# Linear attention and two feed-forward layers: decay products by two long scans per tile, the state kept scaled

## The chip, the cores and the metric

The kernel runs on one core of a Trainium2 chip. TensorE (PE, its weight loads PEld), VectorE (DVE), ScalarE (ACT) and GpSimd (POOL) each work through their own queue in order; SyncE (SP) issues DMAs. The metric is device time in microseconds (us), and a profiled execution gives the trace.

## The reference

A linear attention with a decay per channel runs over 768 steps of 4 sequences and 8 heads of width 48. Its output, 3072 rows of 384, passes two feed-forward layers (FFN).

```python
for t in range(S):                                   # S = 768, D = 48
    cur = einsum('bhd,bhe->bhde', u * k[t], v[t])
    y[t] = einsum('bhd,bhde->bhe', r[t], state + cur)
    state = w[t][..., None] * state + einsum('bhd,bhe->bhde', k[t], v[t])
x = y as rows                                        # 3072 x 384
h = x @ w_in;  x = (h * clip(h + 3, 0, 6) / 6) @ w_out          # d_ff 2048
h = x @ w_in2; s = h * softmax(h); x = layernorm(s) * g_ln @ w_out2   # d_ff 1024
```

The decays w of the inputs lie between 0.8 and 0.95. The weights come as 64-bit floats and are decoded on the chip.

## The kernel before

**Tiles.** The sequence is cut into chunks of 128 steps. A tile is one chunk of one sequence: 6 chunks by 4 sequences make 24 tiles, numbered chunk first, so that tiles 0 to 3 are the first chunk of the four sequences and tile i+4 follows tile i in time. Four tiles of one chunk make a group, and a group feeds 16 FFN slots of 512 columns; slot n multiplies with block m = n mod 16 of the first FFN's weights.

**Stages of a tile.** `stw` clamps the decays to 0.75 to 1.25 (tile wc; on VectorE for tiles 0 to 3, on GpSimd after) and lets ScalarE add up how far any decay lies outside (tile junk), which in the end picks a fallback. `st0` turns w and r (tiles wt, rt in PSUM, by TensorE for tiles 0 to 9, by a VectorE transpose, `flip`, for tiles 10 to 23) and makes the decay products: q by four backward scans of 128 (one for each pair of heads), its reciprocal at the chunk's start, e by four forward scans of 127, and then e times rt. `st1` multiplies q with the turned keys (kt) and makes z = r k u on GpSimd (tile r), whose sum d is taken on VectorE. `keys_in` turns q k back (ktp, ktok), `scores` makes the score products (pa) and the masked scores: GpSimd writes the diagonal (am), VectorE copies pa over it (L630). `state_add` makes the new state, `out_x` the tile's output yt and its high and low parts xh and xl.

**State.** `state_in` makes, on GpSimd, sp = state times the chunk's whole decay (the first column of q) and sr, the columns 32 to 48 of the same. `out_x` multiplies e with sp and sr, and `state_add` adds the keys' product to sp (L649).

**FFN and decode.** `ffn_in` makes h (L720), t and gh (L724 to L726), `ffn_low` gl (on GpSimd in slots 0 to 15, on VectorE after); `ffn_out` follows two slots later (L745), and after a group's last slot ScalarE writes ye (L751) and issues its three stores (L752). Block m of the weights is loaded by `w1_load` (three buffers, raw), decoded on ScalarE (L63) and VectorE (L66, L50, L53), and split (ScalarE L71, VectorE L72). From slot 0 on, one block is decoded in each slot until all 16 are done.

**Order.** SP's queue is in the order of the code, as is GpSimd's until the first FFN slot; the other engines' instructions, and GpSimd's from then on, are put in order by the scheduler that builds the kernel. Every engine then keeps its order, so that an instruction that waits holds all behind it.

After 96 slots the second FFN (L950, L964, L977) goes over the 24 tiles with rows that `load_y` reads back.

Of the kernel before, what the change touches and what calls it, by code (L numbers as in the profile page):

```python
# [278 lines left out]
def fast_path(  # L279
# [107 lines left out]
    at = {}  # L387
    x_t = {}
# [102 lines left out]
    def stw(i):  # L491
        a = at[i]
        if i >= LATE:
            x = late["w"][:, :, 0:4 * D - 16]
            junk = atp.tile([P, HP, 4 * D - 16], mybir.dt.uint8, tag="junk", name="junk", bufs=1)
            nc.scalar.activation(
                out=junk, in_=x, func=ACTF.Relu, scale=-1.0, bias=b_lo, accum_out=chk[:, 3 * i:3 * i + 1]
            )
            nc.scalar.activation(
                out=junk, in_=x, func=ACTF.Relu, bias=b_hi, accum_out=chk[:, 3 * i + 1:3 * i + 2]  # L500
            )
            nc.gpsimd.tensor_scalar(out=x, in0=x, scalar1=W_HI, scalar2=W_LO, op0=ALU.min, op1=ALU.max)
# [8 lines left out]
        a["wc"] = wc  # L511
        junk = atp.tile([P, H, D], BF16, tag="junk", name="junk", bufs=1)
# [7 lines left out]
    def st0(i):  # L520
        a = at[i]
        g = i // B
        if i < LATE:
            wt = ps_in(i, "wt", "y0")
            trans(wt, a["wc"])
            rt = ps_in(i, "rt", "y1")
            trans(rt, a["r"])
        else:
            wt, rt = flip("w"), flip("r")
        q = atp.tile([P, HP, C + 1], F32, tag="q", name="q")  # L530
        e = atp.tile([P, HP, C], F32, tag="e", name="e")
        nc.gpsimd.memset(q[0:DP, :, C:C + 1], 1.0)
# [12 lines left out]
        a.update(q=q, e=e)  # L545

    def st1(i):
# [6 lines left out]
        else:  # L554
            kt = flip("k")
# [8 lines left out]
    def state_in(i):  # L564
        a = at[i]
        b = i % B
        q = a["q"]
        sp = atp.tile([P, HP, 2 * D], F32, tag="sp", name="sp", bufs=1)
# [3 lines left out]
        sr = atp.tile([P, HP, 32], F32, tag="sr", name="sr", bufs=1)  # L572
        nc.gpsimd.tensor_tensor(
            out=sr[0:DP].rearrange("p h (j d) -> p h j d", j=2),
            in0=s_st[b][0:DP].rearrange("p h (j d) -> p h j d", j=2)[:, :, :, 32:D],
            in1=q[0:DP, :, 0:1].unsqueeze(3).to_broadcast([DP, HP, 2, D - 32]), op=ALU.mult,
        )
        a["sp"], a["sr"] = sp, sr
# [53 lines left out]
    def state_add(i):  # L632
# [5 lines left out]
        for h in range(H):  # L638
# [97 lines left out]
    def ffn_out(n):  # L736
# [118 lines left out]
    for tick in range(starts[-1] + NS):  # L855
# [8 lines left out]
        for m in decodes.get(tick, []):  # L864
# [17 lines left out]
    for n in range(NSLOT + LAG):  # L882
# [45 lines left out]
    load_y(0)  # L928
    load_y(1)
# [113 lines left out]
```

## Time and profile before

| what | value |
|---|---|
| median of 3 runs | 775.6 us (774.93 to 776.07) |
| the profiled execution | 774.71 us, span 772.6 us |
| PE busy | 733.3 us (95%) |
| DVE busy | 535.1 us (69%) |
| ACT busy | 333.1 us (43%) |
| POOL busy | 266.3 us (34%) |
| granted TensorE clock, mean | 0.971 of full speed |

The span runs from the first instruction to the last; 2.1 us of the profiled time lie around it. Busy times overlap. A slice of the page is a fortieth of the span, 19.3 us: TensorE is at 5 to 8 tenths in the first seven slices, and at 9 or more in nearly all the others.

### The profile page before, as it was taken

To read this page: it belongs to the slowest core of one execution; us is meant where nothing else is said; L and a number is where in the kernel's file an instruction comes from. 1 tells how busy PE (TensorE), PEld (TensorE's weight loads), DVE (VectorE), ACT (ScalarE), POOL (GpSimd) and SP (SyncE) were. 2 spreads that over 40 slices of the span, in tenths; PEclk is the share of its full clock that TensorE was granted. 3 is DMA by queue.
4 is the path that set the end of the run, shared out by engine and by line. 5 is a ranking of instruction groups with operands and counts; after the bars stand their busy time and mean duration, and the time that the engine had idled before them with its cause. 6 is when DMAs were issued, how large, how long until landed. Compare 5 with 4: busy or idle time off the path is not lost. (4 is left out here: it accounts for less than half of the span.)

```text
span 772.6 us, 14109 instructions
## 1 busy us (share of the span) xinstructions
PE 733.3 (95%) x5308; PEld 620.9 (80%) x5308; DVE 535.1 (69%) x1012; ACT 333.1 (43%) x647; POOL 266.3 (34%) x397
## 2 busy tenths in 40 slices
PE   5778797999999999999999999999999999999996
PEld 4556685888887888878888888888899999999995
DVE  6979889658777777777787865787555555555552
ACT  3455456334434333433334334654444444444442
POOL 5556547742332333333333311224322222222200
PEclk9669998999999999999999999999999999999998
DMA  9794754534344344443335203422111111111001
GB/s 168 172 172 124 178 133 101 108 86 97 86 95 121 86 104 87 93 117 82 91 74 130 63 1 103 144 94 70 65 48 44 41 42 48 45 42 42 31 22 36
DMA packets 151405, 67.31 MB, mean 87 GB/s; under 512 B 101792, under 2 KB 145952, under 8 KB 151328
## 3 DMA queue, kind: packets, MB, share of 16 engines
q1 hardware_dynamic: 148736, 61.60, 33.6%
q10 hardware_dynamic: 2592, 4.72, 1.6%
q8 instruction: 44, 0.72, 0.4%
q14 instruction: 33, 0.27, 0.1%
HBM read 56.33 MB, written 9.44 MB: 85 GB/s over the span
## 5 line engine op out<-in xcount | busy, mean ns | idle before, releaser
L745 PE MATMUL y<-gh,w_h 128*128 128x512 f32 x288 | 115.8, 402 | 0.0
L720 PE MATMUL h<-xh,w_h 128*128 128x512 f32 x288 | 113.4, 394 | 0.0
L720 PE MATMUL h<-xl,w_h 128*128 128x512 f32 x288 | 113.1, 393 | 0.0
L745 PE MATMUL y<-gl,w_h 128*128 128x512 f32 x288 | 113.1, 393 | 0.0
L745 PE MATMUL y<-gh,w_l 128*128 128x512 f32 x288 | 113.0, 392 | 0.0
L720 PE MATMUL h<-xh,w_l 128*128 128x512 f32 x288 | 112.7, 391 | 0.0
L726 ACT ACTIVATE gh<-t 128x512 fp32r<-128x512 f32 x96 | 60.4, 629 | 116.4 <-DVE t L725 116.4
L724 ACT ACTIVATE t<-h,cols 128x512 f32<-128x512 f32 x96 | 65.2, 680 | 93.2 <-PE h L720 91.2
L725 DVE SCALAR_TENSOR_TENSOR t<-t,h 128x512 f32<-128x512 f32 x96 | 65.1, 678 | 34.6 <-ACT t L724 34.3
L734 DVE TENSOR_TENSOR gl<-t,gh 128x512 fp32r<-128x512 f32 x80 | 66.7, 834 | 24.1 <-ACT gh L726 19.1
L78 DVE TENSOR_REDUCE nm<-h 128x1 f32<-128x1024 f32 x24 | 29.4, 1225 | 61.5 <-PE h L950 61.4
L977 PE MATMUL po<-w_oh,qh 128*128 128x384 f32 x192 | 67.2, 350 | 0.3 <-ACT qh L966 0.3
L745 PEld LDWEIGHTS y<-gh,w_h 128*128 128x128 f32 x288 | 54.3, 189 | 13.9 <-issue 3.2
L977 PE MATMUL po<-w_oh,ql 128*128 128x384 f32 x192 | 64.8, 337 | 0.1
L977 PE MATMUL po<-w_ol,qh 128*128 128x384 f32 x192 | 64.8, 338 | 0.0
L745 PEld LDWEIGHTS y<-gh,w_l 128*128 128x128 f32 x288 | 54.5, 189 | 11.8
L720 PEld LDWEIGHTS h<-xh,w_h 128*128 128x128 f32 x288 | 54.6, 190 | 11.5
L720 PEld LDWEIGHTS h<-xh,w_l 128*128 128x128 f32 x288 | 54.6, 190 | 11.4
L720 PEld LDWEIGHTS h<-xl,w_h 128*128 128x128 f32 x288 | 54.6, 190 | 11.3
L745 PEld LDWEIGHTS y<-gl,w_h 128*128 128x128 f32 x288 | 54.6, 190 | 10.4
L966 ACT ACTIVATE qh<-pt 128x512 fp32r<-128x512 f32 x48 | 26.1, 595 | 78.4 <-PE pt L964 78.4
L950 PE MATMUL h<-w_ih,yl 128*128 128x512 f32 x144 | 56.4, 392 | 0.0
(132 smaller groups left out, 1482.6 us busy)
## 6 DMA issues: line engine op xcount, KB each, us to landing
raw<-in_moe_w_out_dram SPq DMA_DIRECT2D x24, 384.0 KB, 6.2
raw<-in_moe_w_in_dram SPq DMA_DIRECT2D x48, 128.0 KB
r<-in_r_dram SPq DMA_DIRECT2D x24, 192.0 KB, 3.0
k<-in_k_dram SPq DMA_DIRECT2D x24, 192.0 KB, 4.2
y1d<-ye ACTq DMA_DIRECT2D x18, 256.0 KB, 3.2
y<-y1d SPq DMA_DIRECT2D x24, 192.0 KB, 2.7
out_dram<-os SPq DMA_DIRECT2D x24, 192.0 KB, 1.9
v<-in_v_dram SPq DMA_DIRECT2D x20, 192.0 KB, 4.7
```

Source lines behind the costliest of these rows:

```text
L78: nc.vector.tensor_reduce(out=nm, in_=h, axis=AX.X, op=ALU.max, negate=True)
L720: nc.tensor.matmul(out=h, lhsT=a, rhs=b, start=(j == 0), stop=(j == len(ops) - 1))
L724: nc.scalar.activation(out=t, in_=h, func=ACTF.Relu, bias=three)
L725: nc.vector.scalar_tensor_tensor(out=t, in0=t, scalar=6.0, in1=h, op0=ALU.min, op1=ALU.mult)
L726: nc.scalar.activation(out=gh, in_=t, func=ACTF.Copy)
L734: eng.tensor_tensor(out=gl, in0=t, in1=gh.bitcast(F32), op=ALU.subtract)
L745: nc.tensor.matmul(out=y_ps[g][c], lhsT=a, rhs=b, start=(m == 0 and j == 0), stop=(m == M1 - 1 and j == 2))
L950: nc.tensor.matmul(out=h[:, fs], lhsT=a[:, c, :], rhs=b_[:, c, fs], start=(j == 0), stop=(j == len(ops) - 1))
L966: nc.scalar.activation(out=qh[:, ms, :], in_=pt, func=ACTF.Copy)
L977: nc.tensor.matmul(out=po, lhsT=x[:, m, :], rhs=y[:, m, :], start=(n == 0), stop=(n == 3 * M2 - 1))
```

## The change

The decays are no longer clamped; the two sums on ScalarE that watch them stay. For tiles 0 to 9 ScalarE copies the turned decays from PSUM into a buffer in SBUF of 4 rows of 129 with a zero ahead of each row (for the later tiles the transpose writes there). One forward scan over all 516 elements makes e: the zero wipes out the row before, and a 1 added from a second tile, `ends`, starts the next. The reciprocals of the four end products are put into `ends`, and one backward scan in place makes q, now divided by the chunk's whole decay. That decay is kept in a small tile (dk). `out_x` reads the state itself, and `state_in` only copies the columns for sr. `state_add` writes the sum of the old state and the keys' product to sp, and a new function, `state_out`, multiplies it with the chunk's whole decay on GpSimd after the tile's output (for the first chunk, the state itself) and so makes the state that the next chunk reads. The mask's ones are set on GpSimd. The stores of ye go to SP, and the first two `load_y` stand two slots ahead of the end.

```diff
 def stw(i):
-            nc.gpsimd.tensor_scalar(out=x, in0=x, scalar1=W_HI, scalar2=W_LO, op0=ALU.min, op1=ALU.max)
             return
-        wc = atp.tile([P, H, 64], F32, tag="wc", name="wc", bufs=1)
-        flat = slice(0, H * 64 - 16)
-        eng = nc.vector if i < B else nc.gpsimd
-        eng.tensor_scalar(
-            out=wc.rearrange("p h d -> p (h d)")[:, flat], in0=a["w"].rearrange("p h d -> p (h d)")[:, flat],
-            scalar1=W_HI, scalar2=W_LO, op0=ALU.min, op1=ALU.max,
-        )
...
 def st0(i):
+        buf = atp.tile([P, NQ + 1], F32, tag="q", name="q")
+        nc.gpsimd.memset(buf[:, 0:NQ + 1:C + 1], 0.0)
+        q = buf[:, 1:NQ + 1].rearrange("p (h t) -> p h t", h=HP)
+        ef = atp.tile([P, NQ], F32, tag="e", name="e")
+        e = ef.rearrange("p (h t) -> p h t", h=HP)
         if i < LATE:
...
-            trans(wt, a["wc"])
+            trans(wt, a["w"])
             rt = ps_in(i, "rt", "y1")
             trans(rt, a["r"])
+            nc.scalar.activation(out=q[0:DP, :, 0:C], in_=wt[0:DP], func=ACTF.Copy)
         else:
-            wt, rt = flip("w"), flip("r")
...
-        for hp in range(HP):
-            nc.vector.tensor_tensor_scan(
-                out=q[0:DP, hp, 0:C][:, ::-1], data0=wt[0:DP, hp, :][:, ::-1], data1=ones[0:DP, :],
-                initial=1.0, op0=ALU.mult, op1=ALU.mult,
-            )
-        nc.vector.reciprocal(out=e[0:DP, :, 0], in_=q[0:DP, :, 0])
-        for hp in range(HP):
-            nc.vector.tensor_tensor_scan(
-                out=e[0:DP, hp, 1:C], data0=wt[0:DP, hp, 0:C - 1], data1=ones[0:DP, 0:C - 1],
-                initial=e[0:DP, hp, 0:1], op0=ALU.mult, op1=ALU.mult,
-            )
-        nc.vector.tensor_tensor(out=e[0:DP], in0=rt[0:DP], in1=e[0:DP], op=ALU.mult)
+            flip("w", q[:, :, 0:C])
+        nc.vector.memset(ends[0:DP, 0:NQ:C + 1], 1.0)
+        nc.vector.tensor_tensor_scan(
+            out=ef[0:DP], data0=buf[0:DP, 0:NQ], data1=ends[0:DP, 0:NQ], initial=1.0, op0=ALU.mult, op1=ALU.add
+        )
+        nc.vector.reciprocal(out=ends[0:DP, C + 1:NQ + 1:C + 1], in_=e[0:DP, :, C])
+        nc.vector.tensor_tensor_scan(
+            out=buf[0:DP, 1:NQ + 1][:, ::-1], data0=buf[0:DP, 1:NQ + 1][:, ::-1], data1=ends[0:DP, 1:NQ + 1][:, ::-1],
+            initial=1.0, op0=ALU.mult, op1=ALU.add,
+        )
...
+        nc.vector.tensor_copy(out=decay[0:DP], in_=e[0:DP, :, C])
+        nc.vector.tensor_tensor(out=a["e"][0:DP], in0=rt[0:DP], in1=a["e"][0:DP], op=ALU.mult)
...
 def state_in(i):
-        nc.gpsimd.tensor_tensor(
-            out=sp[0:DP], in0=s_st[b][0:DP], in1=q[0:DP, :, 0:1].to_broadcast([DP, HP, 2 * D]), op=ALU.mult
+        nc.gpsimd.tensor_copy(
+            out=sr[0:DP].rearrange("p h (j d) -> p h j d", j=2),
+            in_=s_st[i % B][0:DP].rearrange("p h (j d) -> p h j d", j=2)[:, :, :, 32:D],
         )
...
 def state_add(i):
-                nc.vector.tensor_tensor(out=dst, in0=src, in1=a["sp"][o:o + D, :, f:f + D], op=ALU.add)
+                nc.vector.tensor_tensor(out=sp[o:o + D], in0=src, in1=st, op=ALU.add)
...
+    def state_out(i):
+        g, b = divmod(i, B)
+        decay = decays.pop(i)
+        if g == NG - 1:
+            return
+        for j in range(2):
+            o, f = 64 * j, D * j
+            st = s_st[b][o:o + D, :, f:f + D]
+            nc.gpsimd.tensor_tensor(
+                out=st, in0=at[i]["sp"][o:o + D] if g else st,
+                in1=decay[o:o + D].unsqueeze(2).to_broadcast([D, HP, D]), op=ALU.mult,
+            )
...
-                lhs = a["sp"][0:DP, q, D * c:D * c + 32] if c < 2 else a["sr"][0:DP, q, :]
+                lhs = s_st[b][0:DP, q, D * c:D * c + 32] if c < 2 else a["sr"][0:DP, q, :]
...
-                nc.scalar.dma_start(out=y1d[g, :, c, :], in_=ye[:, c, :])
+                nc.sync.dma_start(out=y1d[g, :, c, :], in_=ye[:, c, :])
```

The change also moves instructions. On ScalarE at the start, where tiles 0 and 1 begin (junk: the watch on the decays; ktok, s_st: the keys turned back and the first state of tile 0), this stood there before:

```order
L513 ACT_TABLE_LOAD
L513 ACTIVATE junk,chk<-w,cols 128x384
L516 ACTIVATE junk,chk<-w,cols 128x384
L513 ACTIVATE junk,chk<-w,cols 128x384
L516 ACTIVATE junk,chk<-w,cols 128x384
L589 ACTIVATE ktok<-ktp 128x448
L513 ACTIVATE junk,chk<-w,cols 128x384
```

and now:

```order
L506 ACT_TABLE_LOAD
L506 ACTIVATE junk,chk<-w,cols 128x384
L509 ACTIVATE junk,chk<-w,cols 128x384
L526 ACTIVATE q<-wt 112x4x128
L506 ACTIVATE junk,chk<-w,cols 128x384
L509 ACTIVATE junk,chk<-w,cols 128x384
L581 ACTIVATE ktok<-ktp 128x448
L646 ACTIVATE s_st_114<-kv 48x4x48 x2
L526 ACTIVATE q<-wt 112x4x128
```

The copy of tile 0's decays stands behind its two sums, and that of tile 1's behind tile 0's ktok and state.

On ScalarE where tile 3 ends and tile 4 begins (ktok, s_st and xh are tile 3's; the first junk is tile 4's; dec and w_h belong to the weights' decode), before:

```order
L589 ACTIVATE ktok<-ktp 128x448
L513 ACTIVATE junk,chk<-w,cols 128x384
L71 ACTIVATE w_h<-dec 128x768
L516 ACTIVATE junk,chk<-w,cols 128x384
L651 ACTIVATE s_st_119<-kv 48x4x48 x2
L63 ACTIVATE dec,chk<-raw 128x768
L513 ACTIVATE junk,chk<-w,cols 128x384
L71 ACTIVATE w_h<-dec 128x768
L690 ACTIVATE xh,chk<-yt 128x3x128
```

and now:

```order
L581 ACTIVATE ktok<-ktp 128x448
L71 ACTIVATE w_h<-dec 128x768
L646 ACTIVATE s_st_120<-kv 48x4x48 x2
L506 ACTIVATE junk,chk<-w,cols 128x384
L63 ACTIVATE dec,chk<-raw 128x768
L509 ACTIVATE junk,chk<-w,cols 128x384
L526 ACTIVATE q<-wt 112x4x128
L71 ACTIVATE w_h<-dec 128x768
L700 ACTIVATE xh,chk<-yt 128x3x128
```

The split of weight block 1 (the first w_h) and tile 3's state moved ahead of tile 4's first junk.

On VectorE in slots 5 to 7, around tile 5's masked scores (d, am), before:

```order
L599 TENSOR_REDUCE d<-r 128x8
L72 TENSOR_TENSOR w_l<-dec,w_h 128x768
L630 COPY_PREDICATED am<-causal,pa_934 128x512
L630 COPY_PREDICATED am<-causal,pa_935 128x512
L50 SCALAR_TENSOR_TENSOR dec<-dec,raw 128x768
```

and now:

```order
L591 TENSOR_REDUCE d<-r 128x8
L50 SCALAR_TENSOR_TENSOR dec<-dec,raw 128x768
L72 TENSOR_TENSOR w_l<-dec,w_h 128x768
L622 COPY_PREDICATED am<-causal,pa_918 128x512
L622 COPY_PREDICATED am<-causal,pa_919 128x512
```

Two decode steps now stand between d and the first am, where one stood. On GpSimd at the same place, before:

```order
L532 MEMSET q 112x4
L627 TENSOR_TENSOR am<-ident,d 128x512
L734 TENSOR_TENSOR gl<-t,gh 128x512
L627 TENSOR_TENSOR am<-ident,d 128x512
L399 MEMSET r 128x8x16
```

and now:

```order
L517 MEMSET q 128x5
L744 TENSOR_TENSOR gl<-t,gh 128x512
L619 TENSOR_TENSOR am<-ident,d 128x512 x2
L402 MEMSET r 128x8x16
L744 TENSOR_TENSOR gl<-t,gh 128x512
```

The slot's gl no longer stands between the tile's two am.

## Rows read from the trace of the kernel before

**Rows 1.** Busy time by stretch: PE, PEld, DVE, ACT, POOL, clock, DMA, GB/s.
```profile
0.00:20.00 20.00, 11.44 (x106) 9.22 (x106) 13.49 (x38) 7.14 (x18) 10.39 (x32) 1.00 0.97 171
20.00:50.00 30.00, 22.13 (x225) 16.75 (x226) 27.25 (x48) 15.43 (x37) 15.19 (x22) 0.58 0.81 162
50.00:145.00 95.00, 81.17 (x608) 64.92 (x611) 81.95 (x131) 48.24 (x94) 56.99 (x58) 0.92 0.56 133
145.00:545.00 400.00, 397.90 (x3187) 329.28 (x3176) 292.15 (x533) 168.49 (x332) 132.31 (x194) 1.00 0.38 92
545.00:772.00 227.00, 220.65 (x1199) 200.69 (x1197) 120.25 (x265) 93.81 (x168) 51.37 (x92) 0.99 0.13 42
```

**Rows 2.** Waits of TensorE from 60 to 145 us: total, times, longest.
```profile
PE rt L489 <- issue: 7.6, 3, 4.6
PE ktp L587 <- DVE q L558: 5.1, 2, 4.1
```

**Rows 3.** Groups of instructions, whole kernel: busy us and mean ns, then idle before.
```profile
L540 DVE TENSOR_TENSOR_SCAN e<-wt,e,ones 112x127 f32<-112x127 f32 x96 | 39.8, 463 | 0.6
L534 DVE TENSOR_TENSOR_SCAN q<-wt,ones 112x128 f32<-112x128 f32 x96 | 33.2, 403 | 4.2 <-PE wt L489 3.7
L538 DVE RECIPROCAL e<-q 112x4 f32<-112x4 f32 x24 | 4.2, 176 | 0.5
L507 DVE TENSOR_SCALAR wc<-w 128x496 f32<-128x496 f32 x4 | 2.9, 723 | 2.8 <-DMA w<-in_w_dram 2.8
L589 ACT ACTIVATE ktok<-ktp 128x448 f32<-128x448 f32 x20 | 10.8, 538 | 6.2 <-PE ktp L587 6.0
L507 POOL TENSOR_SCALAR wc<-w 128x496 f32<-128x496 f32 x6 | 5.2, 873 | 5.6 <-DMA w<-in_w_dram 3.7 <-PE wt L489 1.5
L569 POOL TENSOR_TENSOR sp<-s_st,q 112x384 f32<-112x384 f32 x20 | 20.0, 999 | 57.2 <-PE yt L662 53.4 <-DVE s_st L649 3.7 <-DVE q L534 0.2
```

**Rows 4.** Timelines, tile 4's start to tile 6's load: start, duration, idle before and its releaser.
```profile
38.18 3.00 SPq L400 DMA_DIRECT2D k<-in_k_dram  x1
42.18 0.61 ACT L513 ACTIVATE junk<-w,cols 128x384 bf16<-128x384 f32 x1 [3.04 <-DMA w<-in_w_dram]
42.24 0.60 POOL L507 TENSOR_SCALAR wc<-w 128x496 f32<-128x496 f32 x1 [3.74 <-DMA w<-in_w_dram]
43.66 1.44 DVE L72 TENSOR_TENSOR w_l<-dec,w_h 128x768 fp32r<-128x768 f32 x1 [2.09 <-ACT w_h L71]
49.72 1.22 PE L720 MATMUL h<-xh,w_h 128*128 128x512 f32 x2
60.76 0.62 ACT L513 ACTIVATE junk<-w,cols 128x384 bf16<-128x384 f32 x1 [1.31 <-DMA w<-in_w_dram]
68.56 0.91 ACT L63 ACTIVATE dec<-raw 128x768 f32<-128x768 f32 x1 [2.03 <-DMA raw<-in_moe_w_out_dram]
```

**Rows 5.** VectorE's timeline: q times kt of tiles 5, 6, 7; am of tile 5.
```profile
75.98 0.68 DVE L558 TENSOR_TENSOR q<-kt,q 112x512 f32<-112x512 f32 x1
82.23 0.76 DVE L630 COPY_PREDICATED am<-causal,pa 128x512 f32<-128x512 int32 x1 [0.94 <-POOL am L627]
84.49 0.74 DVE L630 COPY_PREDICATED am<-causal,pa 128x512 f32<-128x512 int32 x1 [1.50 <-POOL am L627]
103.02 0.68 DVE L558 TENSOR_TENSOR q<-kt,q 112x512 f32<-112x512 f32 x1
131.06 0.68 DVE L558 TENSOR_TENSOR q<-kt,q 112x512 f32<-112x512 f32 x1
```

**Rows 6.** Busy time by stretch between those, columns as in rows 1.
```profile
76.00:103.00 27.00, 21.73 (x165) 17.56 (x166) 24.04 (x38) 13.85 (x27) 14.62 (x16) 0.87 0.59 147
103.00:132.00 29.00, 23.61 (x184) 19.02 (x183) 25.52 (x40) 16.12 (x33) 16.00 (x15) 0.97 0.60 142
```

**Rows 7.** One line's durations, ns: shortest/median/longest (L53 up to 100 us).
```profile
L540 DVE TENSOR_TENSOR_SCAN e<-wt,e,ones x96: 447/456/482, 8.5 to 441.0; 112x127 f32<-112x127 f32 x96
L53 DVE SCALAR_TENSOR_TENSOR dec<-raw,dec x9: 933/945/2028, 27.2 to 89.7; 128x768 int32<-128x768 int32 x9
```

More of the change, by code (lines that the diff above doesn't have):

```diff
@@ L337, in fast_path @@
     actp = right.enter_context(tc.tile_pool(name="actp", bufs=1, side="right"))
-    ones = actp.tile([P, P], F32, name="ones")
-    nc.vector.memset(ones, 1.0)
+    NQ = HP * (C + 1)
+    ends = actp.tile([P, NQ + 1], F32, name="ends")
+    nc.vector.memset(ends, 0.0)
     causal = actp.tile([P, P], I32, name="causal")
+    nc.gpsimd.memset(causal.bitcast(F32), 1.0)
     nc.gpsimd.affine_select(
-        out=causal.bitcast(F32), in_=ones, pattern=[[1, P]], compare_op=ALU.is_gt, fill=0.0, base=0,
+        out=causal.bitcast(F32), in_=causal.bitcast(F32), pattern=[[1, P]], compare_op=ALU.is_gt, fill=0.0, base=0,
         channel_multiplier=-1,
@@ L387, in fast_path @@
     at = {}
+    decays = {}
     x_t = {}
@@ L458, in load_late, with flip @@
         at[i]["vt"] = t
-    def flip(nm):
-        t = ps_tile(nm + "t")
+    def flip(nm, t):
         nc.vector.transpose(
@@ L501, in stw @@
             )
-            nc.gpsimd.tensor_scalar(out=x, in0=x, scalar1=W_HI, scalar2=W_LO, op0=ALU.min, op1=ALU.max)
             return
-        wc = atp.tile([P, H, 64], F32, tag="wc", name="wc", bufs=1)
-        flat = slice(0, H * 64 - 16)
-        eng = nc.vector if i < B else nc.gpsimd
-        eng.tensor_scalar(
-            out=wc.rearrange("p h d -> p (h d)")[:, flat], in0=a["w"].rearrange("p h d -> p (h d)")[:, flat],
-            scalar1=W_HI, scalar2=W_LO, op0=ALU.min, op1=ALU.max,
-        )
-        a["wc"] = wc
-        junk = atp.tile([P, H, D], BF16, tag="junk", name="junk", bufs=1)
+        junk = atp.tile([P, H, D], mybir.dt.uint8, tag="junk", name="junk", bufs=1)
         nc.scalar.activation(
@@ L528, in st0 @@
         else:
-            wt, rt = flip("w"), flip("r")
-        q = atp.tile([P, HP, C + 1], F32, tag="q", name="q")
-        e = atp.tile([P, HP, C], F32, tag="e", name="e")
-        nc.gpsimd.memset(q[0:DP, :, C:C + 1], 1.0)
-        for hp in range(HP):
-            nc.vector.tensor_tensor_scan(
-                out=q[0:DP, hp, 0:C][:, ::-1], data0=wt[0:DP, hp, :][:, ::-1], data1=ones[0:DP, :],
-                initial=1.0, op0=ALU.mult, op1=ALU.mult,
-            )
-        nc.vector.reciprocal(out=e[0:DP, :, 0], in_=q[0:DP, :, 0])
@@ new lines, in st0 @@
+        nc.vector.reciprocal(out=ends[0:DP, C + 1:NQ + 1:C + 1], in_=e[0:DP, :, C])
[3 more added lines that the diff above has]
+        )
+        if i >= LATE:
+            rt = flip("r", ps_tile("rt"))
+        decay = atp.tile([P, HP], F32, tag="dk", name="dk", bufs=4)
+        nc.vector.tensor_copy(out=decay[0:DP], in_=e[0:DP, :, C])
@@ L547, in st1 @@
+        a.update(q=q, e=e[:, :, 0:C])
+        decays[i] = decay
+        nc.vector.tensor_tensor(out=a["e"][0:DP], in0=rt[0:DP], in1=a["e"][0:DP], op=ALU.mult)
     def st1(i):
@@ L554, in st1 @@
         else:
-            kt = flip("k")
+            kt = flip("k", ps_tile("kt"))
         if 0 < g and i < JOIN:
@@ L565, in state_in @@
         a = at[i]
-        b = i % B
-        q = a["q"]
-        sp = atp.tile([P, HP, 2 * D], F32, tag="sp", name="sp", bufs=1)
-        nc.gpsimd.tensor_tensor(
-            out=sp[0:DP], in0=s_st[b][0:DP], in1=q[0:DP, :, 0:1].to_broadcast([DP, HP, 2 * D]), op=ALU.mult
-        )
[L572 to L578, printed above, removed]
+        sr = atp.tile([P, HP, 32], F32, tag="sr", name="sr", bufs=1)
+        nc.gpsimd.tensor_copy(
+            out=sr[0:DP].rearrange("p h (j d) -> p h j d", j=2),
+            in_=s_st[i % B][0:DP].rearrange("p h (j d) -> p h j d", j=2)[:, :, :, 32:D],
+        )
+        a["sr"] = sr
     def keys_in(i):
@@ L643, in state_add @@
             )
+        if g > 0:
+            sp = atp.tile([P, HP, D], F32, tag="sp", name="sp")
         for j in range(2):
             o, f = 64 * j, D * j
-            dst = s_st[b][o:o + D, :, f:f + D]
             src = kv[o:o + D, :, 0:D]
+            st = s_st[b][o:o + D, :, f:f + D]
             if g > 0:
-                nc.vector.tensor_tensor(out=dst, in0=src, in1=a["sp"][o:o + D, :, f:f + D], op=ALU.add)
-            else:
-                nc.scalar.activation(out=dst, in_=src, func=ACTF.Copy)
+                nc.vector.tensor_tensor(out=sp[o:o + D], in0=src, in1=st, op=ALU.add)
+                a["sp"] = sp
+            else:
+                nc.scalar.activation(out=st, in_=src, func=ACTF.Copy)
+    def state_out(i):
[5 more added lines that the diff above has]
+            o, f = 64 * j, D * j
+            st = s_st[b][o:o + D, :, f:f + D]
+            nc.gpsimd.tensor_tensor(
+                out=st, in0=at[i]["sp"][o:o + D] if g else st,
+                in1=decay[o:o + D].unsqueeze(2).to_broadcast([D, HP, D]), op=ALU.mult,
+            )
     def out_x(i):
-        a = at.pop(i)
+        a = at[i]
         g, b = divmod(i, B)
@@ L681, in out_x @@
             inter(2, False)
+            state_out(i)
+        at.pop(i)
         if b == 0:
@@ L868, in fast_path @@
             w1_a(m)
+    for i in range(B):
+        state_out(i)
     order.close()
@@ L923, in fast_path @@
                 w2_load(j + 2)
+        if n == NSLOT - 2:
+            load_y(0)
+            load_y(1)
         if NA < n < NSLOT:
@@ L927, in fast_path @@
             w2_a(j)
-    load_y(0)
-    load_y(1)
     order.close()
```

1 line of the change is left out of this document (removed).

## The prediction

> **What bounds the kernel now.** I read the busy times by stretch first. From 145 to 545 us TensorE is busy 397.90 of 400 us, and after that 220.65 of 227 [rows 1]: there TensorE's own work is the time, the change takes none of it away, and what other engines save there buys at most the 2.1 us it idles before 545. So the question is the first 145 us, in which TensorE idles 8.6, 7.9 and 13.8 us, at a mean clock of 0.58 from 20 to 50 and 0.92 after. In those two stretches VectorE is busy 27.25 of 30 and 81.95 of 95 us: it is the bound, with transfers beside it (the DMA share is 0.97 and 0.81 in the first two stretches). TensorE's waits say the same: for q, which VectorE makes (5.1 us), and "issue", 7.6 us, of which the page names no releaser [rows 2]. Those are rt transposes; their PSUM buffer is the one that the tile before used for kv, which `state_add` on VectorE frees, and in VectorE's queue that add stands behind decode work. So a microsecond that VectorE saves before 145 us counts almost in full, until transfers or TensorE's own 81 us take over.
>
> **The change, part by part.** *Scans.* The eight scans of a tile cost 33.2 + 39.8 = 73.0 us over 24 tiles, 3.04 a tile [rows 3]. The trace has no scan of 516. From below: VectorE's products of 512 with one input in PSUM take 0.68 us [rows 5]; no scan here is faster per element, so 0.7. From above: 403 ns x 516/128 = 1.62 us. Between them I split the scan's own row: a VectorE instruction on 4 elements takes 176 ns, so 124 more elements cost 227 ns, 1.83 each, and 516 cost 0.176 + 512 x 1.83 = 1.11; I take 1.15, two make 2.3. The reciprocal stays. New are a memset of `ends` and a copy of the decay, 4 elements each, between 0 and 0.18 us apiece; I take 0.12. Net: 2.3 + 0.24 - 3.04 = -0.5 us a tile on VectorE (between -1.6 and +0.5).
>
> The Trainium skill ("DVE: opcode table, instruction layouts, handler registers and perf-mode slots", section Datapath and trigger behaviour) says that the built-in scan runs at half throughput. With its clock of 0.96 GHz that is an estimate of 1.08 us for 516 elements beside the fixed part, 1.25 in all, and the saving would be 0.3 us a tile.
>
> *Clamps.* VectorE loses four of 0.72 us, GpSimd six of 0.87 in tiles 4 to 9 [rows 3] (and those of the late tiles, where nothing waits).
>
> *The copy to SBUF* is new, on ScalarE, which is about half busy [rows 1]. Its price lies by ktok, a copy of 448 from PSUM: 0.54 us; I take 0.6. It is ahead of every first scan, but more important is where it stands. In tile 0 it follows two junk sums, and the scans end when they did: the clamp and the copy cancel. For tile 1 it now stands behind tile 0's ktok and state, and VectorE has the scan behind tile 0's am. An estimate by walking through both queues: tile 0's q k is ready at 11.3 us, ktp and pa hold TensorE to about 14.2, kv and the state's copies to 15.4, tile 1's copy to 16.0. VectorE has nothing but d and am to do from 11.3 on, waits some 2.6 us, and needs 4.2 more to tile 1's q k (2.3 for scans, 0.2, and 0.6 each for e, xl and q k, rounded): 20.2, where 19.3 stood. After that it is never without work, and three missing clamps of 0.72 and three times 0.5 make the 0.9 late into about 2.5 early at tile 3's am; of which I count 1.5, since ScalarE and TensorE (at half clock) are in the chain too.
>
> *State.* GpSimd drops sp, 1.00 us for 384 columns [rows 3]; sr, 128 columns, is copied where it was multiplied; two products of 192 columns are new: between half of sp's row and the whole, 0.5 to 1.0 each, I take 0.6. With the clamp gone its load falls by about 0.7 us a tile. The eight products of the first group come in a row, some 5 us, where GpSimd now waits for turned rows; without that cover the z of tile 4 would be up to 5 us later, and with it its sum d on VectorE. The reads of the state itself need the product of four tiles earlier, 16 slots before: nothing.
>
> *Tile 4's first transfer.* This is the largest single piece. Before, w of tile 4 lands at 42.2; ScalarE (junk) and GpSimd (clamp) both stand waiting for it, and behind them the split of weight block 1 and tile 3's am [rows 4]. VectorE loses 2.09 us there, and the first FFN slot starts at 49.72. Now the split stands ahead of that junk, and no clamp is ahead of am. The transfers themselves come no earlier, as SP's queue is full. TensorE still takes wt and then, newly, rt and kt of tile 4 before slot 0; k's issue ends at 41.2 [rows 4], and I take 45 for its landing, an estimate. So slot 0 starts at about 47: -2.7 us, the lead of tile 3 included.
>
> *Tile 4 to tile 5.* ScalarE used to stand before junk of tile 6 at 60.76 with t of a slot and a decode step behind it [rows 4]; these are now ahead of it. But w of tile 6 still lands at 60.7, tile 4's xh and tile 5's copy still wait for it, and weight block 6 (loaded behind tile 6's rows) still lands about 68.5 [rows 4]. From 60.76 junk (0.8 with its sum), xh and the copy take ScalarE to 62.7; from there VectorE has two scans (2.3), the small ones (0.2), e, t and q k (0.6 each) and four decode steps (three of 0.9, one of 0.5): 7.5 us, so tile 5's q k starts near 69.8 and not before block 6 has landed, where 75.98 stood [rows 5]. 1.2 us back for decode steps that GpSimd holds up: -5 us so far, slot 0's 2.7 included.
>
> *Tiles 6 and 7.* From one q k to the next pass 27.0 and 28.0 us [rows 5], of which VectorE is busy 24.0 of 27 and 25.5 of 29 [rows 6]. In the first it waits 0.94 and 1.50 us for GpSimd's am [rows 5]. Now d has two decode steps behind it and the two am follow each other on GpSimd: I leave 0.3 of the 2.44. With -0.5 for scans the spans become about 24.4 and 25.2 (TensorE's 21.7 and 23.6 us, part of them at the lower clock, are no floor yet): -2.6 and -2.8, and 0.5 us of both back since the longer scans take two inputs from SBUF. Near 140 us TensorE takes over, and the lead stays.
>
> *ye stores, load_y, mask.* Nothing: the stores wait on SP for ye where the next loads wait in any case for buffers freed slots later, and TensorE has no wait near 545 to lose. If that cover were gone, it would cost the stores' landing, 3 us, once.
>
> Sum: -5.0 - 2.6 - 2.8 + 0.5 = -9.9, with 0 to 1 us more where TensorE no longer idles long enough to fall to the lower clock. That is -10.5 on the profiled 774.71, so 764.2; the median of the runs shown is 0.9 above the profiled one, so **765**.
>
> **The rivals.** *Transfers are the floor.* Up to 68 us SP's queue is full, and if w of tile 6 and weight block 6 pin tile 5 to where it was but for 2 us, the sum is -2 - 2.6 - 2.8 + 0.5 = -7, and less if loads also pace the later blocks: 768 to 771. For it: the share of 0.97 and 0.81. Against: after 50 us it is 0.56. Chance 0.12.
>
> *Scans that wait for GpSimd.* Every scan now reads two inputs in SBUF. Scans with one in PSUM never took over 482 ns, while a decode step with two in SBUF reached 2028 against a median of 945 [rows 7]. GpSimd is busy half of the time here, so a scan may wait for one of its instructions, up to 1 us. If each of the 16 scans of tiles 0 to 7 lost 0.45, that is 7 us: 771 to 773. L53's mean loss in these rows, with seven of nine near the median, is more like 0.13, which I have taken in. The Trainium skill has the rule ("SBUF — State Buffer", section Who interferes with whom): a VectorE instruction with two SBUF inputs contends with a GpSimd one that reads SBUF, and the later of the two waits for the whole of the other; the trace agrees, by the row just named. Chance 0.09.
>
> *The copy makes a new wait; slower.* If VectorE stands waiting for ScalarE's copy in each of tiles 1 to 7 as I expect it in tile 1, 2.6 us each, six more cost 15.6, and -10.5 turns into +5: 780. It decides from 1.75 us a tile on. For it: ScalarE's junk waits for transfers, and the copy of the next tile stands behind. Against: from tile 5 on VectorE has decode steps to do between state and scan. Chance 0.05.
>
> *Nothing happens*, as TensorE is 95% busy and the front's idle time only moves into its other waits: 774 to 776. Chance 0.05.
>
> **How the numbers follow.** The forecast has 0.69 with its own range of 758.5 to 769: 3 us below if the long stalls of TensorE go and its clock stays up, and 3 more if the scans are near 0.7; above, scans at 1.62 cost 0.94 a tile and, with tiles 5 to 7 counting, some 3 us. The range, 758.5 to 772, takes in the first rival and half of the second. A measurement here tells 0.2%, 1.55 us, from no change: faster is below 774.0. Forecast, first rival and nearly all of the second: 0.89; the fourth and the rest of the second: 0.06; the third: 0.05.
>
> **What would show it.** Two scans of 516 a tile at 1.1 to 1.25 us, some of them longer by a GpSimd instruction; first FFN matmul at about 47 us; tile 5's q k at about 71, tile 6's near 95 and tile 7's near 121; am without waits of 1 us; TensorE's idle time before 145 us down from 30 to about 20; the stretch after that of the same length. I am wrong if scans take 1.6 us or more, if VectorE idles before each tile's first scan, or if the first slot starts where it did.

## The result, and the profile after

The changed kernel takes 779.99 us (median of 6 runs, 779.24 to 781.72), the kernel before 775.70 on the same chip: a ratio of 1.0061, interval 1.0048 to 1.0074. It is slower by 0.6%, where 765 us was forecast. The profiled execution has a span of 778.3 us. The busy times by stretch say where the loss is (columns as in [rows 1]):

```profile
0.00:20.00 20.00, 13.22 (x99) 9.23 (x100) 9.99 (x23) 8.76 (x21) 11.50 (x35) 1.00 0.98 169
20.00:50.00 30.00, 20.84 (x203) 15.59 (x201) 25.03 (x38) 12.97 (x32) 14.54 (x22) 0.64 0.77 160
50.00:145.00 95.00, 79.03 (x586) 63.08 (x585) 87.32 (x114) 50.28 (x99) 60.01 (x58) 0.90 0.55 131
145.00:545.00 400.00, 398.58 (x3204) 329.59 (x3203) 289.09 (x474) 170.51 (x333) 135.12 (x195) 1.00 0.38 92
545.00:772.00 227.00, 226.15 (x1224) 205.23 (x1222) 120.91 (x266) 95.90 (x172) 51.38 (x92) 1.00 0.13 42
```

From 145 us on TensorE is as full as it was. What came is more work left for the last stretch: 226.15 us of it where 220.65 stood [rows 1], in a fixed window of 227 us, because less was done by 145 us (in the first three rows together, 888 matmuls instead of 939). From 50 to 145 us VectorE is busy 87.32 us instead of 81.95 with 114 instructions instead of 131: fewer and together longer. Before 50 us it is busy less, 35.02 us where 40.74 stood [rows 1], as clamps are gone and waits are new. The groups (busy us and mean ns, then idle before) show which:

```profile
L530 DVE TENSOR_TENSOR_SCAN e<-q,ends 112x516 f32<-112x516 f32 x24 | 34.2, 1425 | 6.2 <-ACT q L526 6.2
L534 DVE TENSOR_TENSOR_SCAN q<-q,ends 112x516 f32<-112x516 f32 x24 | 31.5, 1313 | 0.0
L541 DVE COPY dk<-e 112x4 f32<-112x4 f32 x24 | 6.7, 279 | 0.0
L526 ACT ACTIVATE q<-wt 112x512 f32<-112x512 f32 x10 | 5.9, 589 | 2.3 <-PE wt L491 2.2
```

The two scans cost 65.7 us where 73.0 stood [rows 3], but with very unlike instructions: one line's durations in tiles 0 to 7 (shortest/median/longest), where [rows 7] had 447 to 482 ns for the short form:

```profile
L530 DVE TENSOR_TENSOR_SCAN e<-q,ends x8: 1222/1606/2069, 7.2 to 130.3; 112x516 f32<-112x516 f32 x8
L534 DVE TENSOR_TENSOR_SCAN q<-q,ends x8: 1215/1390/1909, 9.4 to 133.6; 112x516 f32<-112x516 f32 x8
L541 DVE COPY dk<-e x8: 135/262/1078, 8.7 to 132.7; 112x4 f32<-112x4 f32 x8
```

An undisturbed scan takes 1.22 us, within the 1.1 to 1.25 of the forecast. Ten of the 16 are longer than that, and all 16 together by 4.9 us. What lengthens the others is seen in the timelines of tile 3, VectorE and then GpSimd (start, duration):

```profile
33.76 2.07 DVE L530 TENSOR_TENSOR_SCAN e<-q,ends 112x516 f32<-112x516 f32 x1
35.76 0.93 DVE L72 TENSOR_TENSOR w_l<-dec,w_h 128x768 fp32r<-128x768 f32 x1
36.70 1.08 DVE L541 COPY dk<-e 112x4 f32<-112x4 f32 x1
...
33.72 1.02 POOL L559 TENSOR_TENSOR r<-r,k 128x384 f32<-128x384 f32 x1
34.82 2.74 POOL L560 TENSOR_TENSOR r<-r,u_bc 128x384 f32<-128x384 f32 x1
```

GpSimd's product starts at 33.72, the scan at 33.76: the scan ends 1.09 us after that product does (35.83 and 34.74). GpSimd's next product, 1.00 us where nobody is in its way, starts at 34.82 and takes 2.74: it lasts through the rest of the scan and the w_l behind it. The copy of four numbers, 0.14 elsewhere, ends at 37.78, just behind that product's 37.56. So an instruction of one engine stands until a whole one of the other is done; not in strict turn, as the w_l got in ahead of the product that had started before it. The Trainium skill ("SBUF — State Buffer", section Who interferes with whom) has this: a VectorE instruction with two SBUF inputs and a GpSimd one that reads SBUF exclude each other, and plain copies can be in it too; these rows agree, by 2.07 for 1.22, 2.74 for 1.00 and 1.08 for 0.14.

Tile 3's q times kt, before and now, shows how late VectorE is by then, 4.97 us:

```profile
35.94 0.68 DVE L558 TENSOR_TENSOR q<-kt,q 112x512 f32<-112x512 f32 x1
...
40.91 0.69 DVE L557 TENSOR_TENSOR q<-kt,q 112x512 f32<-112x512 f32 x1
```

The second place is tile 4, GpSimd and then VectorE, with the idle time before and its releaser, where [rows 4] shows the old stall:

```profile
46.14 0.11 POOL L517 MEMSET q<- 128x5 f32 x1 [8.40 <-PE pa L597]
46.48 2.31 POOL L619 TENSOR_TENSOR am<-ident,d 128x512 f32<-128x512 f32 x2
48.75 7.52 POOL L656 TENSOR_TENSOR s_st<-s_st,dk 48x192 f32<-48x192 f32 x8
57.84 1.00 POOL L560 TENSOR_TENSOR r<-r,u_bc 128x384 f32<-128x384 f32 x1
...
53.86 1.53 DVE L530 TENSOR_TENSOR_SCAN e<-q,ends 112x516 f32<-112x516 f32 x1
58.87 0.55 DVE L591 TENSOR_REDUCE d<-r 128x8 f32<-128x384 f32 x1 [3.48 <-POOL r L560]
60.08 1.56 DVE L534 TENSOR_TENSOR_SCAN q<-q,ends 112x516 f32<-112x516 f32 x1
62.14 0.68 DVE L557 TENSOR_TENSOR q<-kt,q 112x512 f32<-112x512 f32 x1
```

GpSimd idles 8.40 us and then does the first group's eight state products in a row, 7.52 us. Tile 4's z stands behind them, its sum d behind z, and in VectorE's queue d stands ahead of tile 4's backward scan: 3.48 us in which VectorE does nothing. TensorE's waits of 60 to 145 us (total, times, longest) have a new row, h for t, which is that same stall seen from the FFN:

```profile
PE rt L491 <- issue: 8.2, 2, 6.5
PE h L730 <- DVE t L735: 5.0, 1, 5.0
PE ktp L579 <- DVE q L557: 2.5, 1, 2.5
```

The first FFN matmul and q times kt of tiles 5 to 7 answer to [rows 4, 5]; all are later, by 3.15, 5.99, 4.75 and 6.92 us:

```profile
52.87 0.71 PE L730 MATMUL h<-xh,w_h 128*128 128x512 f32 x2
...
81.97 0.68 DVE L557 TENSOR_TENSOR q<-kt,q 112x512 f32<-112x512 f32 x1
107.77 0.68 DVE L557 TENSOR_TENSOR q<-kt,q 112x512 f32<-112x512 f32 x1
137.98 0.68 DVE L557 TENSOR_TENSOR q<-kt,q 112x512 f32<-112x512 f32 x1
```

### The profile page after: what moved, and what is told of

It reads as the page before. It is cut to its first block, busy times and chain, and to the rows that moved or that the text cites. A ratio compares the mean times of both kernels' runs of the same rounds, so it can differ in the third digit from the quotient of the medians.

```text
span 778.3 us, 14014 instructions
## 1 busy us (share of the span) xinstructions
PE 737.8 (95%) x5308; PEld 622.7 (80%) x5308; DVE 532.3 (68%) x912; ACT 338.8 (44%) x657; POOL 272.5 (35%) x398
## 4 chain that ended last, share of the span: by engine, by line
PE 87%; DVE 6%; issue 2%; DMA 2%; POOL 1%; ACT 1%; SPq 0%; DVEq 0%; POOLq 0%; ACTq 0%
PE y L755 25%; PE h L730 23%; PE h L963 13%; PE po L990 13%; PE pt L977 3%; PE yt L677 2%; PE yt L670 2%; PE pa L597 1%; PE late_pa L611 1%; DMA raw<-in_moe_w_in_dram 1%; PE ktp L579 1%; DVE q L534 1%; DVE e L530 1%; PE kv L632 1%; POOL s_st L656 1%
## 5 line engine op out<-in xcount | busy, mean ns | idle before, releaser
L744 DVE TENSOR_TENSOR gl<-t,gh 128x512 fp32r<-128x512 f32 x80 | 62.5, 781 | 30.0 <-ACT gh L736 28.8
L97 POOL TENSOR_TENSOR st<-st,cols 128x1 f32<-128x1 f32 x24 | 13.2, 550 | 124.0 <-DVE st L94 124.0
```

The source lines that it names most:

```text
L744: eng.tensor_tensor(out=gl, in0=t, in1=gh.bitcast(F32), op=ALU.subtract)
```

## The experiments

The theories. **A**, or *d*: the row of eight state products, through z and d, is the loss. **B**: the copy and the long scans are; and within B *wait* (VectorE or ScalarE's queue pays for the copy), *lock* (two SBUF inputs against GpSimd) and *length* (two long scans gain nothing here at all). Each ratio is against the kernel before on the same chip in the same batch (774.95, 775.16 and 775.34 us in the three batches).

**State products at the end of each tile** (the changed kernel, edited):

```diff
+                if s == NS - 1:
+                    state_out(i)
...
-    for i in range(B):
-        state_out(i)
```

> The changed kernel, with one edit: the first group's eight state products are issued on GpSimd tile by tile, each pair after its own tile's output, and not all eight in a row after tile 3. Theory A (the eight products, 7.5 us in a row ahead of tile 4's z, are what holds VectorE for 3.5 us and TensorE for 5.0 us near 60 us): q times kt of tile 4 moves from 62.1 to about 58, the 5 us wait of TensorE on t goes, and the whole becomes 775 to 776.5. Rival B (the long scans and their copy make tiles 1 to 3 late, and the rest only follows): the first FFN slot stays near 52.9 and the whole gains 1 us or less, 779.

Measured: 779.51 us, 1.0059 (1.0037 to 1.0081). The changed kernel's own loss, unmoved. The forecast of theory A alone is missed, but the run doesn't decide against it: the trace shows that the stall was moved rather than removed. At tile 4 d no longer waits; at tile 1, GpSimd now does two products ahead of z, and VectorE stands there:

```profile
15.98 1.08 POOL L656 TENSOR_TENSOR s_st<-s_st,dk 48x192 f32<-48x192 f32 x2 [0.87 <-ACT s_st L646]
17.14 1.83 POOL L559 TENSOR_TENSOR r<-r,k 128x384 f32<-128x384 f32 x1
...
20.20 0.55 DVE L591 TENSOR_REDUCE d<-r 128x8 f32<-128x384 f32 x1 [2.04 <-POOL q L517]
```

Tile 1's q times kt comes at 23.40, 1.90 later than in the changed kernel, tile 4's at 62.09, the same, and the first FFN slot at 55.23, 2.36 later.

**No clamps** (the kernel before, without the clamps of w; trans reads w itself; else unchanged).

```diff
-        eng.tensor_scalar(
-            out=wc.rearrange("p h d -> p (h d)")[:, flat], in0=a["w"].rearrange("p h d -> p (h d)")[:, flat],
...
-            trans(wt, a["wc"])
+            trans(wt, a["w"])
```

> The kernel before, with the clamps of the decays left out and nothing else (the two watching sums stay). By the prediction's own terms four clamps of 0.72 us leave VectorE, and neither GpSimd's clamp nor the split of weight block 1 waits for tile 4's transfer: 2 to 4 us less, 772 to 774. Rival: other waits take over in the first 50 us, 775 to 776.

Measured: 771.40 us, 0.9947 (0.9926 to 0.9968), 0.6 us under the forecast of 772 to 774. This part of the change is worth 4 us, and the first FFN slot comes at 47.78 instead of 49.72.

**Short scans in the changed kernel** (no copy by ScalarE, eight scans from PSUM, forward ones first; scaled state and stores kept):

```diff
-            nc.scalar.activation(out=q[0:DP, :, 0:C], in_=wt[0:DP], func=ACTF.Copy)
...
+        for hp in range(HP):
+            nc.vector.tensor_tensor_scan(
+                out=e[0:DP, hp, 1:C + 1], data0=wt[0:DP, hp, :], data1=ends[0:DP, 0:C],
+                initial=1.0, op0=ALU.mult, op1=ALU.mult,
+            )
```

> The changed kernel with its two long scans of a tile and the copy to SBUF taken back: eight scans of 128 with one input in PSUM, forward first, no copy on ScalarE; clamps gone, state and stores as in the change. Rival B (copy and long scans are the loss): tile 3's q times kt, at 40.9 in the changed kernel, is back at 36 or before, no scan takes over 0.5 us, and the whole becomes 768 to 773. Theory A (the eight products are the loss): the products stay, so does most of the loss: 776 to 778.

Measured: 772.19 us, 0.9963 (0.9947 to 0.9979), as rival B has it: tile 3's q times kt is at 33.96 and the longest scan takes 0.48 us. So all of the loss, 1.0061 against 0.9963 or 7.6 us, comes with the long scans and the copy. Beside the run without clamps, 0.9947, the scaled state and the stores cost nothing that shows.

**Stores by SyncE alone** (the kernel before).

```diff
-                nc.scalar.dma_start(out=y1d[g, :, c, :], in_=ye[:, c, :])
+                nc.sync.dma_start(out=y1d[g, :, c, :], in_=ye[:, c, :])
...
+        if n == NSLOT - 2:
+            load_y(0)
+            load_y(1)
```

> The kernel before with only the stores of ye moved to SP and the first two reads of y moved ahead. Both theories: no effect, 775 to 776.5. If it is slower by 2 us or more, the transfers are part of the loss.

Measured: 774.26 us, 0.9988 (0.9972 to 1.0003): nothing that shows. The forecast's 775 to 776.5 is missed by 0.7 us, within the interval.

**Long scans that read PSUM, no copy** (the changed kernel, edited up to tile 9).

```diff
-            nc.scalar.activation(out=q[0:DP, :, 0:C], in_=wt[0:DP], func=ACTF.Copy)
...
+            nc.vector.tensor_tensor_scan(
+                out=ef[0:DP, 4:NQ], data0=wf[0:DP], data1=ends[0:DP, 4:NQ], initial=1.0, op0=ALU.mult, op1=ALU.max
+            )
```

> Up to tile 9 each way one scan of 512 that reads the turned w where it lies in PSUM; no copy to SBUF, and one input in SBUF instead of two. Left out: the scans run over the heads' 512 columns without the column between them, so that the resets stand up to four columns off and the values are not the reference's. Theory wait (VectorE stands for ScalarE's copy) and theory lock (scans with two SBUF inputs wait for GpSimd) agree here: both costs are gone, the scans take about 1.22 us each with none over 1.3, VectorE has some 0.5 us a tile less than with eight short ones, so 767 to 771. Theory length (two long scans are themselves no gain in this front, whatever they read): 775 to 780.

Measured: 774.54 us, 0.9991 (0.9977 to 1.0004). No scan is over 1.22 us, and 5.4 us come back against the changed kernel, but that is 3.5 us short of what wait and lock gave, and nearest to length. The trace offers another reason, which this run doesn't test. In VectorE's timeline d of tile 4 waits again, ahead of tile 4's first scan:

```profile
49.21 0.55 DVE L606 TENSOR_REDUCE d<-r 128x8 f32<-128x384 f32 x1 [2.97 <-POOL r L575]
50.54 1.22 DVE L535 TENSOR_TENSOR_SCAN e<-wt,ends 112x512 f32<-112x512 f32 x1
```

And the group of dk's copies in tiles 0 to 7 is longer than it was (348 ns there):

```profile
L556 DVE COPY dk<-e 112x4 f32<-112x4 f32 x8 | 4.8, 594 | 0.0
```

**The copy kept, one input in PSUM** (the changed kernel, edited up to tile 9).

```diff
+            nc.vector.tensor_tensor_scan(
+                out=ef[0:DP, 4:NQ], data0=buf[0:DP, 1:NQ - 3], data1=wf[0:DP], initial=1.0, op0=ALU.mult, op1=ALU.max
+            )
```

> The changed kernel with the copy by ScalarE in its place, and two long scans of 512 up to tile 9 of which one input is the copy in SBUF and the other the turned w in PSUM instead of the column of resets in SBUF. Left out: the second operation is a maximum with w, so the products are not the reference's. Theory lock: no scan over 1.3 us, the 5 us of excess of the sixteen scans of tiles 0 to 7 come back, 773 to 775. Theory wait: the wait for the copy stands as before, 778 to 780.

Measured: 770.34 us, 0.9948 (0.9928 to 0.9968), below what either theory gave. The scans of tiles 0 to 7, with the wait for the copy that is as long as it was (6.2 in the changed kernel):

```profile
L534 DVE TENSOR_TENSOR_SCAN e<-q,wt 112x512 f32<-112x512 f32 x8 | 9.7, 1212 | 5.9 <-ACT q L528 5.9
L543 DVE TENSOR_TENSOR_SCAN q<-q,wt 112x512 f32<-112x512 f32 x8 | 9.5, 1189 | 0.0
```

So *wait* and *length* fall and *lock* stands. But here the order in VectorE's queue differs as well: tile 4's d stands behind its scans and q times kt, so that its wait of 1.80 us holds up less:

```profile
51.11 0.68 DVE L571 TENSOR_TENSOR q<-kt,q 112x512 f32<-112x512 f32 x1
...
53.59 0.55 DVE L605 TENSOR_REDUCE d<-r 128x8 f32<-128x384 f32 x1 [1.80 <-POOL r L574]
```

Two causes had gone at once, 1.0061 against 0.9948 or 8.8 us together; the run with d held back (below) separates them, though not sharply.

**The copy by VectorE** (the changed kernel).

```diff
-            nc.scalar.activation(out=q[0:DP, :, 0:C], in_=wt[0:DP], func=ACTF.Copy)
+            nc.vector.tensor_copy(out=q[0:DP, :, 0:C], in_=wt[0:DP])
```

> The changed kernel with the copy to SBUF by VectorE itself instead of ScalarE, 0.68 us each by the row for its products of 512 with an input in PSUM. Theory wait: VectorE pays 0.7 us a tile but stands for nobody, 5.5 us for 5.5 us at the start plus what the queue of ScalarE costs in tiles 1 to 7; the result is 774 to 778, below the changed kernel. Theory lock: the long scans keep their excess and VectorE has 0.7 us a tile more, 781 to 785.

Measured: 779.16 us, 1.0056 (1.0034 to 1.0077): between the two forecasts, level with the changed kernel. It tells nothing apart by itself. The scans have their excess (1613 and 1407 ns on average), and VectorE waits nowhere for the copy.

**A copy that nobody reads** (the short-scan kernel above).

```diff
+            spare = atp.tile([P, HP, C], mybir.dt.uint8, tag="junk", name="spare", bufs=1)
+            nc.scalar.activation(out=spare[0:DP], in_=wt[0:DP], func=ACTF.Copy)
```

> Short scans as before, from PSUM, without clamps, with scaled state and stores by SyncE, and up to tile 9 a copy of the turned w by ScalarE into a tile that nobody reads (as bytes, 512 columns): ScalarE's time is spent, but no scan waits for it. The same without this copy took 772.2. Theory wait, in the form that only VectorE's standing costs: 772 to 773. In the form that ScalarE's queue itself is late (junk, ktok and state copies behind the 0.6 us): 775 to 778.

Measured: 770.79 us, 0.9947 (0.9927 to 0.9967), against 0.9963 without the copy, and under both forecasts: ScalarE's 0.6 us a tile costs nothing. But one premise of the expectation doesn't hold: the scans do wait for this copy, which reads the same tile in PSUM, although they don't read what it writes. The first scans of tiles 0 and 1 start when it ends, and VectorE idles 6.4 us before them, as it did 6.2 us in the changed kernel:

```profile
7.51 1.36 DVE L529 TENSOR_TENSOR_SCAN e<-wt,ends 112x128 f32<-112x128 f32 x4 [5.90 <-ACT spare L525]
13.16 1.36 DVE L529 TENSOR_TENSOR_SCAN e<-wt,ends 112x128 f32<-112x128 f32 x4 [0.49 <-ACT spare L525]
```

So the run tests both forms of *wait* at once, VectorE's standing and ScalarE's late queue, and clears both.

**d held behind q k** (the changed kernel; a copy of eight numbers of q k into d ahead of the sum, tiles 0 to 9).

```diff
+        if i < LATE:
+            nc.vector.tensor_copy(out=d[0:DP], in_=a["q"][0:DP, 0, C - H + 1:C + 1])
         nc.vector.tensor_reduce(out=d, in_=a["z"], axis=AX.X, op=ALU.add)
```

> The changed kernel with the sum d of each tile up to 9 held behind that tile's q k in VectorE's queue, by a copy of eight numbers of q k into d ahead of it; the long scans keep their two inputs in SBUF. Theory lock alone (the excess of the scans is the whole loss): 778.5 to 780.5. Theory lock and d (half of the loss is the 3.48 us for which VectorE stands at tile 4's d behind the eight state products): 775 to 777, tile 4's q k 3 us or more earlier than at 62.14.

Measured: 777.10 us, 1.0024 (1.0013 to 1.0034), 0.1 us above the range of lock and d and under that of lock alone, and tile 4's q times kt at 56.31 instead of 62.14, with the scans as long as before (1550 and 1504 ns) and d's wait down to 0.91:

```profile
60.04 0.55 DVE L593 TENSOR_REDUCE d<-r 128x8 f32<-128x384 f32 x1 [0.91 <-POOL r L560]
```

The holding copy has a price of its own, for it is lengthened too; two of its eight in the first 145 us take 1.25 us, and three take 0.15 to 0.17:

```profile
L592 DVE COPY d<-q 112x8 f32<-112x8 f32 x8 | 5.6, 698 | 0.0
```

So the stall at d is worth 1.0061 - 1.0024, 2.9 us, net of what the hold costs. With d late in both, the lock is 1.0024 - 0.9948, 5.9 us, but the run with one input in PSUM has no holding copies; the excess of the 16 scans over those of that run is 5.2 us (8 x 3054 ns against 8 x 2401). The sum of the two causes is measured, 8.8 us; how it divides is known only to a few us.

**Long scans from PSUM, the whole computation** (the changed kernel, edited up to tile 9). With decays up to 1 a maximum resets the product as well as a sum does: the product that runs on from the head before is at most 1 going forward, and 1 at a head's end going back, where 1/W is at least 1. That needs no column between heads, so neither buffer nor copy.

```diff
+            nc.vector.tensor_tensor_scan(
+                out=ef[0:DP, 1:HP * C], data0=wf[0:DP, 0:HP * C - 1], data1=ends[0:DP, 1:HP * C], initial=1.0,
+                op0=ALU.mult, op1=ALU.max,
+            )
+            nc.vector.tensor_tensor(out=decay[0:DP], in0=wt[0:DP, :, C - 1], in1=e[0:DP, :, C - 1], op=ALU.mult)
```

> The whole computation, with one long scan each way up to tile 9 that reads the turned w in PSUM, 511 elements, and resets at each head by a maximum in place of a sum, so that no column between heads, no copy by ScalarE and no second large input in SBUF is needed; decays over 1 go to the fallback. Theory lock and d: scans 1.2 us each without excess, the eight state products and d stand as in the changed kernel, so 772 to 775, as in the run that read PSUM in steps of 512. Theory lock alone: 767 to 771.

Measured: 770.80 us, 0.9935 (0.9918 to 0.9953), in the range of lock alone by 0.2 us, though d of tile 4 waits 2.40 us in it. Against the run in steps of 512, 774.54, the scans themselves gain nothing: 1217 and 1208 ns stood there. What the trace has shorter is the decay, which is a product with one input in PSUM here, 150 to 161 ns, where dk's eight copies took 4.8 us:

```profile
L530 DVE TENSOR_TENSOR_SCAN e<-wt,ends 112x511 f32<-112x511 f32 x8 | 9.7, 1214 | 4.2 <-PE wt L491 4.2
L537 DVE TENSOR_TENSOR_SCAN q<-wt,ends 112x511 f32<-112x511 f32 x8 | 10.2, 1269 | 0.0
L534 DVE TENSOR_TENSOR dk<-wt,e 112x4 f32<-112x4 f32 x8 | 1.2, 155 | 0.1
```

That is 3.6 us less on VectorE, against 1.1 us more for a new copy of one number, where the two runs lie 3.7 us apart. No run changes the decay alone, so this reason is not shown; the run with a copy that nobody reads has long dk copies too, 583 ns each, and takes 770.79.

**The same with d held back** (the same two lines).

> The kernel with 511-element scans from PSUM and the maximum, with d held behind q k too. Theory lock and d: both costs gone, 768 to 771. Theory lock alone: the same as without the hold, within 1.5 us.

Measured: 768.87 us, 0.9921 (0.9905 to 0.9937), inside the forecast of lock and d; the step from 0.9935, 1.1 us (1.9 by the medians), is of the expected sign, but the intervals overlap and it is about what lock alone allowed. The holding copies take 5.8 us here, so it too is net of their price.

**The same without the hold, the first group's state scaled as it leaves PSUM.**

```diff
-                nc.scalar.activation(out=st, in_=src, func=ACTF.Copy)
+                nc.vector.tensor_tensor(
+                    out=st, in0=src, in1=decays[i][o:o + D].unsqueeze(2).to_broadcast([D, HP, D]), op=ALU.mult
+                )
```

> The kernel with 511-element scans from PSUM and the maximum, with the first group's state scaled by VectorE as it leaves PSUM (eight products of 192 columns in tiles 0 to 3, 0.35 us each by the rows of sp, 2.8 us in all) in place of ScalarE's copy and of GpSimd's eight products in a row. Theory lock and d: GpSimd's row of products is gone, z of tile 4 is early, d doesn't wait; 4 us back, 2.8 spent: 769 to 773, and below the same kernel without this edit. Theory lock alone: 2 to 3 us above the same kernel without this edit.

Measured: 767.96 us, 0.9907 (0.9892 to 0.9922): the fastest here, 0.9% under the kernel before and 1.5% under the changed one, with the whole computation. VectorE's eight products cost 353 ns each, 2.8 us, and are more than paid back, where lock alone gave a loss of 2 to 3 us. It is 1 us under the range of lock and d. The intervals of this run and of the one without the edit touch, and the edit also takes eight copies off ScalarE, so the step says less about d alone than its sign does. The group of these products:

```profile
L663 DVE TENSOR_TENSOR s_st<-kv,dk 48x192 f32<-48x192 f32 x8 | 2.8, 353 | 3.1 <-PE kv L649 3.0
```

And d of tile 4 in VectorE's timeline, which waits for nobody:

```profile
52.59 0.52 DVE L608 TENSOR_REDUCE d<-r 128x8 f32<-128x384 f32 x1
```

## Why the prediction was wrong

**What held.** The bound: all of the loss arises before 145 us, where VectorE is, and so do the gains but for at most the 2.1 us that TensorE idles from 145 to 545 us. The undisturbed long scan: 1.22 us, near the 1.15 taken. The Trainium skill ("DVE: opcode table, instruction layouts, handler registers and perf-mode slots", section Datapath and trigger behaviour) has the built-in scan at half throughput, which gave an estimate of 1.25; the trace agrees, nearer still. The copy, 0.59 for 0.6, and its place: tile 1's ends at 16.70, where 16.0 was forecast. VectorE's idle time before it, 6.2 us in two pieces, of which the 5.50 at the start are mostly the wait for the first input (4.82 before); it is harmless, as it stands in the run that takes 770.3. The stores, nothing.

**The step that failed first: "0.5 us of both back since the longer scans take two inputs from SBUF".** The cost was put at L53's mean loss, 0.13 a scan, "with seven of nine near the median". Measured were 0.31 a scan, 4.9 us over the 16, and 5.9 us of the kernel's time by the two runs above, holding copies included. The row was wrong for this: the seven L53 near the median all started while GpSimd did nothing, and the two that met its work are the two that were lengthened, to 1.07 and 2.03 us. The scans stand where GpSimd makes the same tile's z, am or state products. Ten of the 16 were lengthened, by 0.16 to 0.85 us. The copies of the decay, priced at 0.12 each, were lengthened as well: 0.35 on average in tiles 0 to 7. The rival "Scans that wait for GpSimd" had the mechanism and nearly the price, 7 us; it missed only the sign, because the 10.5 us that it was set against weren't there. The third rival gave the right time, 780, by luck: its wait is one that the runs clear.

**The second: the cover of the eight state products.** The text had them at 5 us "where GpSimd now waits for turned rows", and named z of tile 4 as what would be late without that cover. GpSimd does idle there (8.40 us), but ahead of tile 3's am, and in its queue the products stand behind that am: they begin when the idle time is over. At 7.52 us, lock included, they made VectorE wait 3.48; 2.9 us by the run with d held back, net of the hold.

**Without both, 770.3 remains where 765 was forecast.** "About 2.5 early at tile 3's am", of which 1.5 counted, did not come: without the lock tile 3's q times kt is at 36.36 where 35.94 stood. In the run with 511-element scans, which has no copy ahead of the first scans, it is at 33.82, 2.1 early; so it is the copy's place at the start that takes the lead. Nor does any run show the lead to be worth time: 770.80 with it, 770.34 without, and of the two runs with short scans the one that has tile 3 at 37.87 is no slower (770.79) than the one that has it at 33.96 (772.19). So the 1.5 us counted for it has no run behind it. And "the spans become about 24.4 and 25.2" did not come either. In the run with 511-element scans and d held back, tiles 5, 6 and 7 follow at 74.25, 100.64 and 127.11, 26.4 us each, and am still waits 0.94 us for GpSimd. VectorE is busy 24.7 and 25.1 us in those two spans, much what it was in [rows 6]; whether by decode steps that move up into them or by more waits for GpSimd, no run separates, so this part, some 5 us, stays open. TensorE's idle time before 145 us, forecast at about 20, is still 26.3 us in the run with one input in PSUM. Of the savings that the text counts, the clamps with the transfer that they waited for are the only ones with a run of their own: 4 us.

The first slot at 47 us failed by the first cause alone: tile 4's transfer is no longer waited for, but tile 3 itself is 5 us late by then (40.91). The state products only come behind tile 3's am; with d held back the slot is still at 52.52, with one input in PSUM at 47.98, and in the run without clamps at 47.78. Of the three signs that were to prove the prediction wrong, scans of 1.6 us or more are there (seven of the 16 of tiles 0 to 7), and the first slot started later than it had.

## What to carry to other kernels

When short VectorE instructions are joined into a long one, the place of its inputs counts as well as its length. Here the long scans with one input in PSUM kept their 1.2 us, and those with both in SBUF beside a busy GpSimd lost more than they saved. Price such a term from instructions that run at the same place in the program as the new one will, and look for a form that leaves one input where it was; here a maximum in place of a sum did. Where work is put on an idle engine, read what releases that idle time: work that stands behind it in the queue doesn't fill it, and what stands behind the work is late.

## What the hardware showed beyond that

A copy of four numbers from SBUF to SBUF, 0.14 us alone, took up to 1.08 us beside GpSimd, while the product of four numbers with one input in PSUM stayed at 150 to 161 ns: even a very small instruction can wait for a whole one of the other engine. Which ones do is not a matter of size alone: the reciprocal of the same four numbers stayed at 165 to 181 ns in tiles 0 to 7, and a copy of one number in the run with 511-element scans at 135 to 154. It works in both directions: GpSimd's product of 384 columns, 1.00 us, took 2.74, and its eight state products 7.52 us in all, 877 ns each on average, where 498 was the shortest.
